# Gated linear attention and an MLP on one core: a fourth pair of units in the one-token layout, more turns by DMA, first states scaled out of PSUM, softplus for three logs, and a new order

## The chip, the core and the metric

The kernel runs on one core of a Trainium2 chip. The metric is the time of the whole program on the device in microseconds (us). Five engines work side by side, each through its own queue in order: TensorE (PE) multiplies matrices into PSUM, VectorE (DVE), ScalarE (ACT) and GpSimd (POOL) do elementwise work, and SyncE (SP) issues transfers, which 16 DMA engines carry out. ACT and DVE read PSUM; POOL and the DMA engines work on SBUF.

## The reference

A gated linear attention, whose output feeds an MLP with SiLU. There are 4 batches, 8 heads, 768 tokens and 48 columns per head; the MLP goes from 384 to 2048 and back.

```python
f = 1.0 / (1.0 + np.exp(-f_logit))
for t in range(S):
    state = f[:, :, t, :, None] * state + np.einsum('bhd,bhe->bhde', k[:, :, t], v[:, :, t])
    y[:, :, t] = np.einsum('bhd,bhde->bhe', q[:, :, t], state)
...
h = x @ w_in
g = h * (1.0 / (1.0 + np.exp(-h)))
return (g @ w_out)
```

Here x is y with the eight heads of a token side by side, 3072 rows of 384.

## The kernel before

**Units and pairs.** The 768 tokens of a batch are cut into six chunks of 128. One batch's chunk is a unit, so there are 24; they are worked in twelve pairs (`PAIRS`, line 19). In a pair of kind N the units are the same chunk of two batches, and each of the 128 partitions holds one token: a head's row in DRAM is 192 bytes. In a pair of kind T the two units are two neighbouring chunks of one batch, and a partition holds two neighbouring tokens (384 bytes); rows 0 to 63 are the first chunk's, and a step with index i takes every second token of both, so each matmul for scores, values or states comes in pieces of 64 rows. Before, pairs 0 to 3 are T (chunks 0 and 1 of the four batches) and pairs 4 to 11 are N.

**Steps of a unit.** The words are those of the plan; P is the pair and i the unit.
- f, k, q, v: loads, of a whole pair or of half of it (line 239, queue of SP).
- E, L: the log of the gate. E is exp(-f) (line 246) and L is ln(1 + E) (lines 258 and 261). Where the plan has L without E, L is one softplus(-f) (lines 249 to 255).
- cs: running sums of the logs along the tokens, by a triangular matrix on PE (lines 317 to 332). ia and a: its exp with both signs (line 334); al: the decay of a whole chunk (lines 276 and 336).
- ki, qg: k and q times these (line 339). vb: v in bf16 (line 341).
- The turned qk: eight PE transposes, tq (line 346), and a copy out of PSUM, qkc (lines 350 and 352); or one DMA transpose, qkD (line 354).
- sc: scores (lines 363 and 367). at: masked scores (line 371). y, and yi for the second unit of a T pair: the output of the unit, from the scores and from the state before it (lines 283, 379, 383). yc: y to bf16.
- d, sd, su: the change of the state (lines 295 and 400), its sum with the state before (line 404; for a first chunk a copy, line 406), and that times the decay (line 414), two instructions of 48x192. Where the plan has su without sd, su reads d in PSUM (line 411).
- The turned y: three PE transposes, yT (line 391), and a copy, xc (line 393); or one DMA transpose, yD (line 395).
- mi, si, mo, oc, so: the MLP. mi is two blocks of 128 of the hidden layer for the pair's 256 tokens (six matmuls, line 269; a third index makes it one unit's 128 tokens), si the SiLU (line 274), mo a quarter of the second product for one unit (four matmuls, line 304), oc the copy out of PSUM, so the store (lines 314 and 316).
- wi, wo: loads of the weights on POOL's queue, with a cast to bf16 (lines 216 and 219). idle: matmuls of zeros, 512 columns each (line 459).

**What sets the order.** `PLAN` (line 37) is a list written out in full, 881 words before. A word is name:engine:slots, where the engine is A (ACT), V (DVE), G (POOL), S (SP) or P (PE), and slots are the buffers taken. Instructions are emitted in this order, so each engine works through its own words in this order and waits at each for what it needs. That holds for SP too: a qkD or yD that waits keeps the loads behind it back. ACT keeps one set of tables at a time: `mode_of` (line 449) tells which of softplus, exp (with ln) and silu a step needs, and line 507 loads the set where it changes.

Of the kernel before, what the change touches and what calls it, by code (L numbers as in the profile page):

```python
# [41 lines left out]
idle.512.3::3 sc.0.0:P:3,7 al.2:A:1 ia.2.0:A:4 su.0.0:G:0 sc.0.1:P:5,1 f.4.0:S:0 at.0.0.1:V:0 E.3.0:A:0 at.0.0.0:V: tq.1.0:P:7 al.1:A:2 a.2.0:A:2
wi.1:G: v.2.0:S:2 at.0.1.0:V:1 tq.1.1:P:2 L.3.0:A:0 qkc.1.1:V:1 qkc.1.0:A: ki.2.1:G:4 idle.512.1::3 cs.3.1:P:3 at.0.1.1:V: cs.3.0:P:4 a.3.1:A:1
ki.2.0:V:0 wi.0:G: sc.1.0:P:5,2 ia.3.1:A:0 at.1.0.0:V:2 y.0:P:7,1 a.2.1:A:3 qg.2.0:G: al.3:A:3 yc.0.0:A:0 at.1.0.1:V: q.3.0:S:3 sc.1.1:P:6,3
vb.1.1:A:2 yi.0.1:P: qg.2.1:G: at.1.1.1:V:3 yT.0.0:P:5 vb.1.0:A:3 tq.2.0:P:7 yc.0.1:A:1 at.1.1.0:V: d.1:P:2,3 a.3.0:A:4 wi.2:G: yT.0.1:P:1 sd.1.0:A:1
tq.2.1:P:6 xc.0.1:V:0 ia.3.0:A:2 xc.0.0:V: su.1.0:G:0 k.3.0:S:3 y.1:P:2,1 qkc.2.0:A:0 sd.0.1:V:0 mi.0.3.0:P:4 yc.1.0:V:2 mi.0.3.1:P: wi.3:G:
qkc.2.1:V: yi.1.1:P: mi.0.2.0:P:5 yc.1.1:A:0 yT.1.0:P:0 su.0.1:G:0 mi.0.2.1:P: xc.1.0:V:1 E.4.0:A:1 yT.1.1:P:7 xc.1.1:V: sc.2.1:P:2,6 sd.1.1:V:1
sc.2.0:P:1,0 L.4.0:A:1 mi.1.2.1:P:7 at.2.1.0:V:0 mi.1.3.1:P:3 mi.1.3.0:P: at.2.0.0:V:1 k.4.0:S:4 mi.1.1.0:P:2 at.2.1.1:V: mi.1.1.1:P: mi.1.2.0:P:
at.2.0.1:V: si.0.2:A:0 mi.0.1.0:P:1 mi.0.1.1:P: si.1.1:A:1 mi.1.0.0:P:6 si.1.2:A: mi.0.0.1:P:5 vb.2.1:G:4 mi.1.0.1:P: vb.2.0:A:5 wo.0:G: mi.0.0.0:P:
# [4 lines left out]
mi.2.2:P:4 si.2.3:A:2 si.1.7:A: tq.3.1:P:7 v.4.0:S:5 si.2.0:A: mi.2.1:P:1 qkc.3.1:V:1 si.0.6:A: mo.0.1.0:P:6 si.2.1:A: vb.3.1:G:6 tq.3.0:P:3
su.2.1:G:0 si.1.6:A: mi.2.5:P:7 qkc.3.0:V: si.1.5:A: mi.2.7:P:2 vb.3.0:G:0 si.2.5:A: wo.3:G: mo.0.0.0:P:1 si.2.7:A: v.5.0:S:0 si.2.2:A: ki.4.1:G:3
d.3:P:5,0 sd.3.0:V:0 sc.3.0:P:3,7 sc.3.1:P:2,4 su.1.1:G:0 at.3.0.1:V:2 mo.0.0.1:P: at.3.1.0:V:3 E.5.0:A:0 mo.2.1.0:P:5 su.3.0:G:0 mo.1.1.0:P:7
L.5.0:A:2 f.6.0:S:2 mo.1.1.1:P: sd.3.1:V:1 at.3.1.1:V: mo.0.0.2:P: at.3.0.0:V: mo.2.1.1:P: y.3:P:2,0 mo.1.1.2:P: q.4.1:S:4 mi.2.6:P:4 mi.2.4:P:3
# [4 lines left out]
vb.5.1:A:2 mo.2.0.3:P: qkD.4.1:S:0 mi.3.1:P:7 oc.2.0:V:3 vb.4.0:V:3 mi.3.0:P:2 si.3.2:A:3 oc.2.1:V:4 si.3.3:A: qg.4.0:V: mo.1.0.2:P: si.3.5:A:
mi.3.6:P:0 q.6.0:S: ki.5.0:G:4 si.3.1:A: f.8.0:S:3 tq.4.0:P:3 si.3.0:A: so.1.1:G: mi.3.4:P:5 vb.4.1:A:4 qg.5.0:V: q.7.0:S:1 vb.6.1:A:5 qg.5.1:V:1
mo.1.0.3:P: si.3.4:A: ki.5.1:G: cs.6.1:P:1 qkc.4.0:A:1 mi.3.7:P:4 cs.6.0:P:7 si.3.7:A: d.4.0:P:2 qkD.5.0:S:2 mo.3.1.0:P:5 sd.4.0:V:0 si.3.6:A:
oc.1.0:V:5 vb.5.0:A:0 mo.3.1.1:P: sc.4.1:P:3,4 sc.4.0:P:2,0 at.4.1.0:V:0 mo.3.1.2:P: qkD.5.1:S:3 a.6.1:A:2 at.4.0.0:V:1 mo.3.0.0:P:6 E.8.0:A:0
# [475 lines left out]
```

## Time and profile before

| what | time |
| --- | --- |
| median of 3 runs | 183.14 us |
| lowest and highest run | 183.08 and 184.12 us |
| the profiled execution | 181.74 us |
| its span, first to last instruction | 179.9 us |
| mean granted TensorE clock | 0.991 of full speed |

The profile shows one execution. Its views are a page (shares of busy time, slices of the span, the chain of work that ended last, groups of like instructions) and answers about the trace: stretches of the span, the chain in order of time, waits, DMA landings. In a group's row, "x32 | 2.4, 219 | 0.0" means 32 instructions, busy 2.4 us together, 219 ns each on average, and 0.0 us during which their engine was idle just before them. "<-" after that names what ended the idle time. "pb" is any of the eight PSUM buffers. Matmuls are pipelined, so 32 of 219 ns fit into 2.4 us.

### The profile page before, as it was taken

The numbers are of one execution on the slowest core, as the hardware profiler recorded it, in microseconds if no ns is written. First come the engines' busy times: TensorE is split into PE (matmuls) and PEld (weight loads), VectorE is DVE, ScalarE is ACT, GpSimd is POOL, SyncE is SP. The second block draws the span as 40 slices with busy tenths as digits, with TensorE's granted clock in tenths as the row PEclk, the third lists the DMA queues.
The fourth block names the chain that finished last, engine by engine and source line by source line (L and its number), as shares of the span: only waits on it lengthen the run. The fifth ranks groups of instructions, "written<-read, shape, count | busy, mean of one in ns | idle before, by whom it ended". The sixth has DMA issues, their size and how long they took to land.

```text
span 179.9 us, 4982 instructions
## 1 busy us (share of the span) xinstructions
PE 170.3 (95%) x2039; PEld 130.0 (72%) x2040; DVE 83.2 (46%) x165; ACT 134.9 (75%) x252; POOL 59.9 (33%) x107
## 2 busy tenths in 40 slices
PE   6978599999999999999999999998999999999992
PEld 2355589998666787679688877787866877887782
DVE  7089977343710263793666064551058758000010
ACT  4899759999936899887997969783896971278321
POOL 6027753695200370140464500581305220003030
PEclk9999879999999999999999999999999999999999
DMA  5999999999989997999949999698985951314043
GB/s 142 315 321 309 202 242 256 230 209 193 180 176 182 203 201 134 210 204 207 158 106 221 178 202 205 125 218 170 216 156 122 213 127 26 109 26 131 0 154 112
DMA packets 109574, 31.91 MB, mean 177 GB/s; under 512 B 103536, under 2 KB 109088, under 8 KB 109552
## 3 DMA queue, kind: packets, MB, share of 16 engines
q1 hardware_dynamic: 104928, 26.19, 69.1%
q0 software_dynamic: 4624, 5.41, 16.0%
q8 instruction: 16, 0.26, 0.6%
q14 instruction: 6, 0.05, 0.1%
HBM read 25.17 MB, written 4.72 MB: 166 GB/s over the span
## 4 chain that ended last, share of the span: by engine, by line
PE 84%; ACT 6%; DVE 3%; DMA 2%; issue 2%; POOL 0%; POOLq 0%; DVEq 0%
PE pb L304 33%; PE pb L269 33%; PE pb L459 3%; DMA xT<-yb 2%; ACT x L334 2%; PE pb L346 2%; PE pb L379 2%; PE pb L383 2%; PE pb L367 2%; DVE atm L371 2%; PE pb L329 2%; DVE qk L339 1%; PE pb L391 1%; PE pb L295 1%; PE pb L363 1%
## 5 line engine op out<-in xcount | busy, mean ns | idle before, releaser
L304 PE MATMUL pb<-w_out_sb,hT 128*128 128x384 bf16 (+1 forms) x416 | 70.7, 313 | 0.1
L269 PE MATMUL pb<-xT,w_in_sb 128*128 128x256 bf16 (+1 forms) x672 | 70.1, 257 | 0.7 <-DMA xT<-yb 0.5
L274 ACT ACTIVATE hT<-pb 128x512 bf16<-128x512 f32 x96 | 51.0, 611 | 23.2 <-PE pb L269 23.1
L269 PEld LDWEIGHTS <-w_in_sb 128*128 128x128 bf16 x672 | 56.9, 98 | 8.2 <-issue 0.9
L304 PEld LDWEIGHTS <-hT 128*128 128x128 bf16 x416 | 37.9, 97 | 18.1
L414 POOL TENSOR_TENSOR st<-sd,al 48x192 bf16<-48x192 f32 x40 | 20.6, 516 | 54.7 <-PE pb L379 18.2
L371 DVE TENSOR_TENSOR atm<-pb,triu 128x512 bf16<-128x512 f32 x32 | 20.0, 682 | 15.2 <-PE pb L367 15.2
L187 DVE COPY ob<-pb 128x384 f32<-128x384 f32 (+1 forms) x16 | 8.3, 526 | 36.0 <-PE pb L304 35.9
L334 ACT ACTIVATE x<-pb 128x384 f32<-128x384 f32 x48 | 22.0, 511 | 3.3 <-PE pb L329 1.5
L507 ACT ACT_TABLE_LOAD x17 | 21.8, 1283 | 0.3
L339 POOL TENSOR_TENSOR qk<-k,x 128x384 bf16<-128x384 f32 x11 | 11.4, 1038 | 14.9 <-DVE vb L187 13.5
L339 DVE TENSOR_TENSOR qk<-k,x 128x384 bf16<-128x384 f32 x13 | 11.9, 936 | 8.3 <-DMA k<-in_k_dram 5.4
L404 DVE TENSOR_TENSOR sd<-pb,st 128x384 f32<-128x384 f32 x16 | 8.6, 550 | 12.6 <-PE pb L400 6.1
L316 POOL DMA_DIRECT2D out_dram<-ob x7 | 4.0, 569 | 29.5 <-ACT ob L185 21.1
L339 DVE TENSOR_TENSOR qk<-q,x 128x384 bf16<-128x384 f32 x17 | 11.4, 688 | 3.3 <-DMA q<-in_q_dram 1.8
L246 ACT ACTIVATE e<-f 128x768 f32<-128x768 f32 (+1 forms) x13 | 10.5, 804 | 2.0 <-DMA f<-in_f_logit_dram 2.0
L185 ACT CAST yb<-pb 128x384 bf16<-128x384 f32 x16 | 7.6, 490 | 3.6 <-PE pb L383 2.4
L371 DVE TENSOR_TENSOR atm<-pb,mask 128x512 bf16<-128x512 f32 x16 | 10.1, 680 | 0.4 <-PE pb L363 0.4
L339 POOL TENSOR_TENSOR qk<-q,x 128x384 bf16<-128x384 f32 x7 | 7.1, 1019 | 7.4 <-ACT x L334 5.8
L459 PE MATMUL pb<-zero,triu 128*128 128x512 bf16 x19 | 7.1, 525 | 1.5 <-POOL triu masks.py:66 1.4
L185 ACT COPY ob<-pb 128x384 f32<-128x384 f32 (+1 forms) x10 | 4.4, 456 | 4.6 <-PE pb L304 4.6
L346 PE MATMUL pb<-ident,qk 128*128 128x128 bf16 x80 | 6.7, 234 | 0.4 <-DVE atm L371 0.4
(72 smaller groups left out, 153.2 us busy)
## 6 DMA issues: line engine op xcount, KB each, us to landing
f<-in_f_logit_dram SPq DMA_DIRECT2D x11, 384.0 KB, 5.5
k<-in_k_dram SPq DMA_DIRECT2D x16, 192.0 KB, 3.7
v<-in_v_dram SPq DMA_DIRECT2D x16, 192.0 KB, 4.3
q<-in_q_dram SPq DMA_DIRECT2D x16, 192.0 KB, 4.2
q<-in_q_dram SPq DMA_DIRECT2D x4, 384.0 KB, 5.2
k<-in_k_dram SPq DMA_DIRECT2D x4, 384.0 KB, 4.9
v<-in_v_dram SPq DMA_DIRECT2D x4, 384.0 KB, 7.3
w_in_sb<-in_moe_w_in_dram POOLq DMA_DIRECT2D x4, 384.0 KB, 7.5
```

What stands on the lines that cost most here:

```text
L185: nc.scalar.copy(dst, src)
L246: return nc.scalar.activation(e, at("f", P)[:, j * w:(j + 1) * w], AF.Exp, scale=-1.0)
L269: nc.tensor.matmul(h[:, i, cols], w_in_sb[:, kk, n * 128:(n + 1) * 128], at("xT", P)[:, kk, cols], start=(kk == 0), stop=(kk == KT - 1))
L274: return nc.scalar.activation(at("hT", P)[:, 2 * j:2 * j + 2, :], at("h", P, j).rearrange("p (n c) -> p n c", n=2), AF.Silu)
L304: nc.tensor.matmul(at("o", P, i)[:, cols], at("hT", P)[:, n, i * C:(i + 1) * C], w_out_sb[:, n, cols], start=(n == 0), stop=(n == NT - 1))
L334: nc.scalar.activation(at(kind, P, i).rearrange("p h d -> p (h d)"), at("cs", P, i)[:, 0:HD], AF.Exp, scale=1.0 if kind == "ia" else -1.0)
L339: ENG[eng].tensor_mul(at("qk", P, i)[:, j, :, 0:D], heads("qk"[j], P, i), at("ia" if j else "a", P, i))
L346: nc.tensor.transpose(t_ps[:, j, p, :], at("qk", P, i)[:, j, 2 * p:2 * p + 2, :], ident)
L371: ENG[eng].tensor_mul(at("atm", P, i)[:, r], at(f"s{r}", P, i).rearrange("p (n c) -> p n c", c=C), mask[:, None, :].to_broadcast([C, NP, C]))
L414: ENG[eng].tensor_mul(at("st", P, i)[lo:lo + D, :, r * D:(r + 1) * D], src[lo:lo + D, :, r * D:(r + 1) * D], al_of(P, i)[lo:lo + D, :, Non ...
L459: nc.tensor.matmul(buf["pb", int(got)][:, 0:rest[0]], triu, zero[:, 0:rest[0]], start=True, stop=True, skip_group_check=True)
L507: nc.scalar.preload_act_table_set(TABLES[mode])
```

## The change

Pair 3 becomes N: the same units, (3,0) and (3,1), that is chunks 0 and 1 of batch 3, with one token per partition. Its four loads become halves, one per unit. `emit` gets a case for a load of one unit, which takes batch and chunk from the unit itself, and a case for qkD of a T pair, which the new plan doesn't use.

The plan is a new one, of 871 words. What is on PE, ACT, DVE, POOL and SP in it, by count before and after:

| steps | before | after |
| --- | --- | --- |
| tq with qkc (turn of qk on PE) | 10 | 6 (pairs 0 to 2) |
| qkD (turn of qk by DMA) | 14 | 18 |
| yT with xc (turn of y on PE) | 12 | 6 |
| yD (turn of y by DMA) | 12 | 18 |
| E on ACT | 13 | 10 (none for pairs 0 to 2) |
| L on ACT | 13 | 14 (softplus for pairs 0 to 2: four) |
| sd on ACT / DVE | 3 / 17 | 0 / 16 (none for the four first chunks) |
| su on POOL / DVE | 20 / 0 | 16 / 4 |
| ki on DVE / POOL | 13 / 11 | 18 / 6 |
| qg on DVE / POOL | 17 / 7 | 14 / 10 |
| vb on ACT / DVE / POOL | 10 / 8 / 6 | 3 / 10 / 11 |
| oc on ACT / DVE | 10 / 16 | 17 / 9 |
| so on SP / POOL | 14 / 12 | 7 / 19 |
| idle matmuls | 20 | 16 |
| table sets that ACT loads, the first included | 18 | 19 |

In the new order the pairs follow one another by number throughout, and most loads of a unit stand one pair ahead of their use. The old order loads further ahead (f.4, k.4 and v.6.1 stand before the first MLP products of pair 2, for instance), and it works pair 8 ahead of pair 7. The core of the diff, with the first lines of both plans:

```diff
-    ('T', (3, 0), (3, 1)),
+    ('N', (3, 0), (3, 1)),
...
-f.0.0:S:0 f.0.1:S: f.2.0:S:1 f.1.0:S:2 q.0.0:S:0 E.0.0:A:0 E.0.1:A: k.0.0:S:0 L.0.0:A:0 L.0.1:A: idle.512.11::0 cs.0.1:P:0 E.2.0:A:1 k.1.0:S:1
-cs.0.0:P:1 ia.0.1:A:0 v.0.0:S:0 E.1.0:A:0 ia.0.0:A:1 q.1.0:S:1 a.0.0:A:2 L.1.0:A:1 qg.0.0:G:0 L.2.0:A:2 f.3.0:S:3 idle.512.5::2 cs.1.1:P:2 ki.0.0:V:
-al.0:A:0 a.0.1:A:3 ki.0.1:V:1 cs.1.0:P:3 ia.1.1:A:4 cs.2.0:P:4 k.2.0:S:2 qg.0.1:V: ia.1.0:A:2 tq.0.0:P:5 ki.1.1:V:2 a.1.0:A:1 cs.2.1:P:6 ki.1.0:V:3
...
+f.1.0:S:0 f.0.1:S:1 f.0.0:S: q.0.0:S:0 k.0.0:S:0 L.1.0:A:0 f.2.0:S:2 L.0.1:A:1 idle.512.9::0 cs.1.1:P:0 L.0.0:A: k.1.0:S:1 cs.1.0:P:1 cs.0.0:P:2
+q.1.0:S:1 cs.0.1:P:3 ia.0.0:A:0 a.0.0:A:1 ki.0.0:V:0 v.0.0:S:0 al.1:A:0 ia.1.0:A:2 qg.0.0:V: a.0.1:A:3 ia.0.1:A:4 qg.0.1:V:1 ia.1.1:A:0 v.1.0:S:1
+idle.512.2::4 tq.0.0:P:4 ki.0.1:V: a.1.0:A:1 qkc.0.0:V:0 a.1.1:A:3 tq.0.1:P:5 ki.1.1:G:2 f.3.0:S:3 qkc.0.1:V: ki.1.0:V:3 L.2.0:A:2 q.2.0:S:2
+idle.512.3::6 sc.0.0:P:6,7 qg.1.0:V: sc.0.1:P:2,1 at.0.0.0:V:0 qg.1.1:G: cs.2.0:P:0 tq.1.0:P:4 k.2.0:S:2 at.0.1.0:V:1 cs.2.1:P:5 wi.1:G: qkc.1.0:V:1
+al.0:A:1 vb.0.1:A:0 tq.1.1:P:6 f.3.1:S: a.2.0:A:4 vb.0.0:G:1 at.0.1.1:V: qkc.1.1:A: vb.1.0:G:2 d.0:P:2,3 at.0.0.1:V: vb.1.1:G:3 v.2.0:S:2 su.0.0:V:0
+a.2.1:A:0 wi.0:G: idle.512.2::4 sc.1.1:P:4,1 ia.2.0:A:2 sc.1.0:P:7,6 at.1.1.1:V:2 E.3.0:A:0 wi.2:G: y.0:P:2,0 at.1.1.0:V: yc.0.0:A:0 yi.0.1:P: wi.3:G:
+yc.0.1:A:1 at.1.0.0:V:3 d.1:P:1,2 ia.2.1:A:1 yT.0.0:P:4 at.1.0.1:V: qg.2.1:G:4 al.2:A:2 L.3.0:A:0 yT.0.1:P:0 xc.0.0:V:0 q.3.0:S:3 cs.3.0:P:7
+su.1.0:V:0 qg.2.0:G:0 y.1:P:5,6 xc.0.1:V: yc.1.0:A:2 yi.1.1:P: sd.0.1:V:0 mi.0.3.0:P:4 al.3.0:A:3 mi.0.2.1:P:1 ki.2.1:V: yT.1.0:P:0 ki.2.0:V:
...
                 w = n * HD
+                if n == 1:
+                    b, c = us[j][0] - j, us[j][1]
...
         elif kind == "qkD":
-            nc.sync.dma_start_transpose(out=at("qkT", P, i).rearrange("p j n c -> p (j n) c"), in_=at("qk", P, i).rearrange("p j h d -> p (j h d)"))
+            if T:
+                dst = at("qkT", P).rearrange("p j n g s c -> p (j n) g s c")[:, :, :, i]
+            else:
+                dst = at("qkT", P, i).rearrange("p j n c -> p (j n) c")
+            nc.sync.dma_start_transpose(out=dst, in_=at("qk", P, i).rearrange("p j h d -> p (j h d)"))
```

A later stretch of the new plan, around the turns of pair 3: `qkD.3.0:S:0 ... v.3.0:S:3 ... v.3.1:S: ... k.3.1:S: ... vb.3.0:V:6 ... d.3.0:P:6 ... ki.3.1:V: ... qkD.3.1:S:1`, in which SP comes to v.3.0, v.3.1 and k.3.1 only behind qkD.3.0. At the end, both plans work the second product of pair 11 in halves of 192 columns, and store these.

More of the change, by code (lines that the diff above doesn't have):

```diff
@@ L42 @@
[L42 to L49, printed above, removed]
@@ L54 @@
[L54 to L57, printed above, removed]
@@ L62 @@
[L62 to L65, printed above, removed]
@@ new lines @@
+so.3.0:G: si.6.3:A: y.7.0:P:2 so.4.1:G: ki.8.0:V:2 mo.6.1.0:P:0 si.6.4:A: yc.7.0:V:0 su.6.1:G:0 mo.6.0.1:P: q.8.1:S: d.7.1:P:5 yD.7.0:S: mo.6.1.1:P:
+sd.7.1:V:0 a.8.0:A:4 mo.6.0.2:P: E.9.0:A:0 qg.8.0:V: mo.6.1.2:P: al.8.1:A:5 qkD.8.0:S:3 al.8.0:A:0 L.9.0:A:0 mo.6.1.3:P: d.7.0:P:4 qg.8.1:V:
+oc.6.1:A:1 v.8.0:S:2 cs.9.0:P:1 cs.9.1:P:2 a.9.0:A:0 mi.7.1:P:5 q.9.0:S:3 ia.9.1:A:1 ia.9.0:A:2 qkD.8.1:S:2 mi.7.0:P:3 a.9.1:A:4 al.9.1:A:4
+mo.6.0.3:P: al.9.0:A:3 sc.8.0:P:6,0 at.8.0.1:V:0 mi.7.6:P:2 k.9.0:S:3 si.7.1:A:3 at.8.0.0:V: mi.7.5:P:1 si.7.6:A: v.8.1:S: vb.8.0:V:1 mi.7.7:P:0
@@ new lines @@
+k.10.0:S: mo.8.0.3:P: L.11.0:A:2 v.10.1:S:4 d.9.1:P:4 mo.8.1.2:P: sd.9.1:V:0 so.2.0:S: qg.10.0:V:2 cs.11.1:P:7 mi.9.7:P:6 ki.10.1:V: cs.11.0:P:2
+oc.8.0:V:3 qkD.10.1:S:3 mi.9.0:P:5 a.11.0:A:1 ia.11.0:A:4 mi.9.1:P:1 a.11.1:A:2 ki.10.0:V: ia.11.1:A:0 mo.8.1.3:P: qkD.10.0:S:2 vb.10.1:V:5 mi.9.4:P:4
+mi.9.2:P:3 q.11.0:S:5 si.9.1:A:2 mi.9.6:P:2 v.10.0:S: si.9.2:A: si.9.0:A: q.11.1:S: mi.9.5:P:7 si.9.7:A: sc.10.1:P:1,3 si.9.6:A: k.11.1:S:5
+at.10.1.1:V:0 mi.9.3:P:5 oc.8.1:A:0 at.10.1.0:V: mo.9.0.0:P:6 si.9.3:A: so.8.1:G: k.11.0:S: qg.11.0:V:4 si.9.4:A: sc.10.0:P:2,3 si.9.5:A:
```

100 lines of the change are left out of this document (51 added, 49 removed).

## The prediction

> **What bounds the kernel now.** I read the page's shares of busy time first, then the slices, then three stretches of the span side by side, then the chain that ended last.
>
> ```profile
> PE 170.3 (95%) x2039; PEld 130.0 (72%) x2040; DVE 83.2 (46%) x165; ACT 134.9 (75%) x252; POOL 59.9 (33%) x107
> PE   6978599999999999999999999998999999999992
> DMA  5999999999989997999949999698985951314043
> ```
>
> TensorE (PE) is the bound by far. The row of slices says where it is not: only the first five of 40 slices (4.5 us each) hold gaps of size. The DMA engines are the second busiest thing, full until the last quarter.
>
> ```profile
> 0.00:25.17 25.17, 19.50 (x285) 12.33 (x287) 17.43 (x47) 19.55 (x41) 11.04 (x29) 0.93 1.06 259
> 25.17:176.77 151.60, 150.78 (x1760) 117.64 (x1754) 65.73 (x119) 115.09 (x212) 48.90 (x79) 1.00 0.84 166
> 176.77:179.90 3.13, 0.00 (x0) 0.00 (x0) 0.00 (x0) 0.31 (x1) 0.00 (x0) 1.00 0.26 84
> ```
>
> Columns: length, then busy us (instructions) of PE, weight loads, DVE, ACT and POOL, then granted clock, DMA share, GB/s. The kernel has three parts: a start of 25.17 us until the first MLP matmul (mi.0.3.0), a dense part in which PE is busy 150.78 of 151.60 us, and a tail of 3.13 us. So a change pays in two ways only: it takes matmuls out of the dense part, or it lets the dense part begin earlier. And it costs where it opens holes in the dense part.
>
> The chain shows what sets the start (start us, length us, what):
>
> ```profile
> 17.26 0.68 DVE atm L371
> 17.94 1.69 DVE qk L339
> 19.63 1.18 issue
> ...
> 36.88 0.17 PE pb L391 x3
> ...
> 41.19 0.45 PE pb L346 x8
> ```
>
> Up to 24.7 us it runs through ACT's exponentials and DVE's masks and products; from there it is PE alone.
>
> **The change part by part.** Counts are from the two plans.
>
> *Turns moved from PE to DMA.* tq goes from 10 to 6, yT from 12 to 6. The chain prices a tq (eight transposes in a row) at 0.45 us and a yT (three) at 0.17. In the order after the first MLP matmul the old plan has 4 tq and 10 yT, the new one 2 and 4: 2 x 0.45 + 6 x 0.17 = 1.9 us less PE. (The other two removed tq show in where the dense part begins.) As bounds, the two groups below give 2.4 / 4 = 0.60 per tq and 3.3 / 10 = 0.33 per yT, latency included: 1.9 to 3.2.
>
> ```profile
> L391 PE MATMUL pb<-ident,yb 128*128 128x128 bf16 x30 | 3.3, 219 | 0.0
> L346 PE MATMUL pb<-ident,qk 128*128 128x128 bf16 x32 | 2.4, 219 | 0.0
> ```
>
> The copies out of PSUM that go with them (four qkc, six xc), three sd and seven vb leave ACT some 8 us lighter in net; ACT is not the bound (115 of 151.6), so I count nothing. The same goes for moved oc, ki, qg and vb.
>
> *Pair 3 in the other layout.* Its score, value and state products become half as many with all rows in use; by the times in the chain these cancel within 0.2 us. I take 0.1 less, so the dense part has **2.0 us** less work in all.
>
> *The start.* Here softplus, the PSUM scaling and the new order act together, so I follow the new order along each engine.
>
> ```profile
> 4.16 0.52 ACT L246 ACTIVATE e<-f 128x384 f32<-128x384 f32 x1 [0.36 <-DMA f<-in_f_logit_dram]
> 7.12 0.49 ACT L334 ACTIVATE x<-pb 128x384 f32<-128x384 f32 x1 [0.42 <-PE pb L326]
> 9.58 1.48 DVE L339 TENSOR_TENSOR qk<-k,x 128x384 bf16<-128x384 f32 x2 [5.36 <-DMA k<-in_k_dram]
> 10.50 2.03 ACT L334 ACTIVATE x<-pb 128x384 f32<-128x384 f32 x5
> L339 DVE TENSOR_TENSOR qk<-k,x x5: 546/550/3023, 9.6 to 17.9; 128x384 bf16<-128x384 f32 x5
> L261 ACT ACTIVATE lf<-e 128x768 bf16<-128x768 f32 x8 | 6.8, 849 | 0.2
> L507 ACT ACT_TABLE_LOAD x17 | 21.8, 1283 | 0.3
> L185 ACT COPY qkTT<-pb 128x1024 bf16<-128x1024 bf16 x3 | 3.3, 1084 | 0.0
> L187 DVE COPY qkTT<-pb 128x1024 bf16<-128x1024 bf16 x5 | 3.4, 687 | 3.6 <-PE pb L346 3.6
> L185 ACT COPY sd<-pb 128x384 f32<-128x384 f32 x3 | 1.5, 512 | 2.2 <-PE pb L295 2.2
> L187 DVE COPY ob<-pb 128x192 f32<-128x192 f32 x2 | 0.7, 358 | 21.4 <-PE pb L304 21.4
> L414 POOL TENSOR_TENSOR st<-sd,al 48x192 bf16<-48x192 f32 x40 | 20.6, 516 | 54.7 <-PE pb L379 18.2 <-DVE sd L404 10.9 <-DVE qk L339 9.1
> 5.00:15.00 10.00, 8.28 (x110) 4.88 (x110) 5.01 (x10) 9.23 (x22) 1.32 (x2) 1.00 1.15 318
> ```
>
> Softplus is not in the trace. The nearest row is Ln on the same 128x768 (0.85 us); the function that it replaces needs Exp and Ln, so between 0 (free) and 1.7 (as dear as both). I take 0.85. Loads of two tokens per partition land one per 0.393 MB / 318 GB/s = 1.24 us. f.1.0, now first and whole, is as many bytes as the two first halves of before, which were in at 4.16. L.1.0 then ends at 5.0, and L.0.0 at about 6.3. A table load to exp (1.28) follows, so the first ia starts at 7.6, against 7.12. Nine operations at 2.03 / 5 = 0.41 us take ACT to 11.3. Softplus's table, L.2.0 and exp's table (3.4) take it to 14.7; al.0, vb.0.1, a.2.0 and the copy qkc.1.1 (1.08) to 16.8.
>
> DVE: k.0.0 is now the fourth such load, not the fifth, so it lands about 1.2 us earlier, near 8.3, and the first product starts there instead of at 9.58. Products at 0.55 us, held to ACT's pace, are done by 10.6; two qkc (0.69) by 12.0; ki.1.0 and qg.1.0 by 13.1, or by 14.0 if POOL's product beside them holds them up. Three at, qkc.1.0 and another at (0.68 each) end the masks of pair 0 at 16.5 to 17.4, against 17.94. Now the old order lost the most: ki.2.0 took 3.02 us, not 0.55, beside POOL's products (the maximum in the row for k above, 1.69 + 1.18 in the chain). The new order puts su.0.0 there, straight from PSUM. A DVE write of 48x192 from PSUM with two inputs isn't shown; I take 0.36 from the copy of 192 columns, bounded by 0.2 and POOL's 0.52. It replaces sd on ACT (0.5) and two su on POOL (1.0) by 0.72 on DVE. Four at (pair 1, waiting for qkc.1.1 until 17.1) end near 20.8, xc.0.0, su.1.0 and xc.0.1 near 22.2, and the first MLP matmul starts near **21.9** instead of 25.17. It isn't dense yet: tq.2.1 and tq.2.0 wait for ki.2.1 and ki.2.0 on DVE, some 1.7 us later, and yT.1.1 for a copy behind them. PE runs without a hole from 24.1 to 25.1, say 24.6, and has then done 2.1 us of the work that before lay behind 25.17. The gain is 25.17 - 24.6 + 2.1 = **2.7 us**. Bounds: 4.0 (no hole after the first MLP matmul, dense from 23.3) and 0.1 (softplus at 1.7 for three pairs, 2.55 us later).
>
> *What the turns cost.* Each qkD waits on SP's queue for ki and qg, and each yD for yc; the loads of v and k for the next units stand right behind them (qkD.3.0, then v.3.0, v.3.1, k.3.1), so a late ki delays vb and d as well.
>
> ```profile
> qkT<-qk SPq DMA_TRANSPOSE x14, 3.5
> DMA to landing us min/median/max: 2.3/2.6/5.8
> ```
> ```profile
> L185 ACT CAST yb<-pb 128x384 bf16<-128x384 f32 x16 | 7.6, 490 | 3.6 <-PE pb L383 2.4
> ```
> ```profile
> 96.81 5.89 PE pb L269 x54
> ...
> 106.97 2.60 PE pb L304 x16
> ```
> ```profile
> PE pb L269 <- DMA xT<-yb: 0.5, 1, 0.5
> ```
>
> qkD takes 3.5 us to land; the second row is yD's. I added up PE's new order between a pair's last y and its first mi, at 0.65 us per group of mi (six matmuls, 5.89 / 9) or mo (four, 2.60 / 4). What is left after a copy of 0.5 us and a landing of 2.6 us is 0.3 to 2.3 us at the boundaries of pairs 3 to 11. Nine boundaries against six, and landings that reach 5.8 us: I take **1.5 us** of new holes; from 0 to 6 (nine times 0.65).
>
> *Fewer idle matmuls, one more table load, stores from POOL, 2 or 3 halves of a load more:* nothing. ACT and POOL have the room, and the tail's last two copies and stores are as before.
>
> *Sum against the profiled execution*, 181.74 us (span 179.9, 1.84 around it): -2.0 - 2.7 + 1.5 = -3.2, so 178.5. The median of the runs, 183.14, lies 1.4 above the profiled one; from it the same sum gives **179.9 us**, rounded to 180.0.
>
> **The rivals.** *The DMA engines become the bound: slower.* Engine time per MB is share x length / bytes:
>
> ```profile
> 50.00:60.00 10.00, 10.00 (x113) 6.74 (x111) 0.96 (x2) 4.98 (x11) 0.00 (x0) 1.00 0.94 186
> 141.50:146.30 4.80, 4.80 (x45) 3.94 (x43) 2.91 (x8) 4.08 (x7) 0.00 (x0) 1.00 0.78 149
> 60.00:130.00 70.00, 69.28 (x755) 53.80 (x752) 34.22 (x64) 58.96 (x115) 26.67 (x43) 1.00 0.96 184
> ```
>
> Loads of one token per partition (50 to 60 us): 0.94 x 10 / 1.86 = 5.05 us per MB; two tokens (5 to 15 us): 1.15 x 10 / 3.18 = 3.6; turns (141.5 to 146.3): 5.2; stores (the tail's row): 3.1. A qkD of 0.262 MB is 1.4 us, a yD of 0.098 MB 0.5. The change adds 4 x 1.4 + 6 x 0.5 = 8.6 and pair 3's loads 1.57 x 1.45 = 2.3: 10.9 us of DMA time. An N pair needs 7.9 + 3.8 + 1.2 = 12.9, and PE spends 151.6 / 12 = 12.6 on a pair. Because the new order loads fewer pairs ahead, pairs 4 to 11, pair 3's turns and early stores, some 106 us, fall between about 46 and 158 us: a share of 0.95. Before, 0.96 was carried from 60 to 130 us with 0.7 us of PE gaps (69.28 busy of 70), and 1.15 was reached; so it should fit, with little over. If SP's waits let only 0.88 through, these stages take 120.5 us, 8.5 more: 183.1 - 4.7 + 8.5 = 186.9. It passes the gain where the share stays below 106 / (112 + 4.7) = 0.91.
>
> *The turns come late: no change.* Each boundary loses 0.5 us instead of 0.17, 4.5 us in all: 183.1 - 4.7 + 4.5 = 182.9. For it: a yD of before took 5.8 us to land. Against: PE waited for xT once in six pairs, 0.5 us in all. The Trainium skill speaks against this part of the change: its page "VectorE: DVE Perf Modes", section "The three transpose paths", gives a 128x128 turn as 390 ns on TensorE and 1309 ns by DMA, and says to use TensorE where PSUM is acceptable. By that rule each of ten moved turns would be a loss. The trace agrees on latency (0.45 us and a copy against 3.5) but not on cost, since PE is the bound.
>
> *The start gives nothing: no change.* If each of the three table loads ahead of qkc.1.1 also drained ACT for as long as it lasts, the chain above would be 3 x 1.28 = 3.8 us longer and all of the 2.7 gone: 183.1 - 2.0 + 1.5 + 1.1 = 183.7. In the trace 17 loads have 0.3 us of idle time before them, so I give it little. The Trainium skill, "ScalarE: Activation LUTs", section "What ACT_TABLE_LOAD costs", has this drain (1380 ns on top of 1283); the row here shows 1283 and no such idle time.
>
> **How the numbers follow.** Forecast 0.60, late turns 0.22, empty start 0.03, DMA bound 0.15. The forecast's own range is 177 to 182. With the rivals the range is 176.8 to 185.3: the lower end is 4.0 at the start, 2.0 of PE work and hardly any hole, and the upper end takes in the late turns and the beginning of the DMA rival, leaving out some 0.15. A measurement here tells 1% (1.8 us) from no change. Faster by more than that (under 181.3): 0.60. Within 1%: 0.25. Slower: 0.15.
>
> **What would show it.** The start: first MLP matmul near 22 us and PE without holes from 24 to 25; softplus near 0.85 us; su on DVE near 0.36; no DVE product of 3 us. The dense part: tq 6, yT 6, and PE's gaps there near 2 us, on xT. The DMA share near 0.95 from 46 to 158 us. Wrong if PE waits for qkT, qk or loads at several pairs, if the share saturates, or if the first MLP matmul is no earlier than 25.

## The result, and the profile after

The changed kernel takes **190.94 us** (median of 4 runs, 190.23 to 191.90) beside 183.63 us for the kernel before on the same chip (4 runs, 183.08 to 184.35): a ratio of 1.040, 95% interval 1.033 to 1.047. It is slower by 7.3 us; the prediction was 180.0 us, in a range to 185.3. The profiled execution took 191.27 us, with a span of 189.5. (Some executions of either kernel are 1 to 2% longer at random; the ratios below leave these out, so a median can lie above ratio times before.)

The page of the changed kernel, first the shares and then the slices (4.7 us each):

```profile
PE 171.8 (91%) x1944; PEld 126.9 (67%) x1944; DVE 78.9 (42%) x166; ACT 130.0 (69%) x242; POOL 60.3 (32%) x109
...
PE   7788856999999999999799999999999989997992
...
PEclk9969997999999999999999999999999999999999
DMA  6999999908989789999799999898999898837004
```

PE's row now dips where it was full: slices 6 and 7 (23.7 to 33.2 us), and in PEclk the seventh slice ran at 0.7 of the clock. (The third ran at 0.6; the kernel before has a loss of that kind in its fifth and sixth, 0.8 and 0.7.) The DMA row, which was nearly all 9 until the last quarter, has an empty slice (the ninth, 37.9 to 42.6 us).

The same three parts as in the prediction, with the dense part cut in three, for after and then for before:

```profile
0.00:21.76 21.76, 17.33 (x263) 10.40 (x264) 15.55 (x48) 16.15 (x30) 11.41 (x29) 0.92 1.01 240
21.76:45.00 23.24, 19.16 (x329) 17.03 (x327) 10.07 (x20) 13.35 (x28) 8.23 (x13) 0.93 0.90 146
45.00:165.00 120.00, 115.94 (x1160) 83.90 (x1158) 49.11 (x91) 92.09 (x170) 36.45 (x59) 1.00 0.97 187
165.00:186.13 21.13, 19.41 (x201) 15.59 (x198) 4.13 (x8) 8.09 (x17) 4.25 (x8) 1.00 0.34 99
```
```profile
25.17:45.00 19.83, 19.83 (x362) 18.41 (x357) 10.07 (x18) 18.73 (x34) 12.52 (x20) 1.00 1.23 221
45.00:155.00 110.00, 109.22 (x1207) 81.35 (x1205) 54.94 (x99) 85.95 (x157) 32.56 (x52) 1.00 0.88 173
155.00:176.77 21.77, 21.73 (x196) 17.87 (x193) 0.71 (x2) 10.40 (x22) 3.83 (x7) 1.00 0.26 80
```

The first MLP matmul does come at 21.76 us (forecast 21.9, before 25.17). But from there to the last matmul it takes 186.13 - 21.76 = 164.4 us instead of 151.6. PE stands idle for 4.08 + 4.06 + 1.72 = 9.9 us of it, as against 0.8 before. Length times GB/s gives the bytes that have moved by 45 us: before 25.17 x 259 + 19.83 x 221 = 10.9 MB, after 21.76 x 240 + 23.24 x 146 = 8.6 MB. The new order is 2.3 MB behind when its dense part has begun. Some 1.5 MB of that are missing from 31 to 45 us (14 us at 101 GB/s instead of 211), around the empty slice.

What PE waited for in the changed kernel (us in total, times, longest):

```profile
PE pb L330 <- ACT lf L262: 4.9, 3, 3.4
PE pb L347 <- DVE qk L340: 2.8, 3, 1.7
PE pb L270 <- DMA xT<-yb: 2.7, 5, 1.4
...
PE pb L372 <- DMA qkT<-qk: 1.0, 2, 0.6
```

The longest wait of the first row, 3.4 us, is cs.3.1, which waits for L.3.1 on ACT. ACT itself stood still: the last load of f ahead of it, f.3.1 (one transfer on SP's queue), is in this answer on the tile f from 14 to 32 us:

```profile
L240 SPq DMA_DIRECT2D f<-in_f_logit_dram x1: 1809/1809/1809, 15.3 to 15.3; - x1
...
  DMA f<-in_f_logit_dram: 4.9, 1
...
DMA to landing us min/median/max: 13.7/13.7/13.7
```

It went out at 15.3 us and landed 13.7 us later; the four halves of f take 4.4 us in the median, the ten whole loads, with twice the bytes, 5.2. What else was on the DMA engines then is in POOL's timeline (start, length), after and before. Lines L215 and L216 are the loads of the first weight matrix, L218 those of the second:

```profile
14.04 0.94 POOL L215 DMA_DIRECT2D w_in_sb<-in_moe_w_in_dram  x1
...
16.32 2.29 POOL L215 DMA_DIRECT2D w_in_sb<-in_moe_w_in_dram  x3
...
26.51 1.54 POOL L218 DMA_DIRECT2D w_out_sb<-in_moe_w_out_dram  x2
```
```profile
15.71 0.95 POOL L216 DMA_DIRECT2D w_in_sb<-in_moe_w_in_dram  x1
...
17.67 0.79 POOL L216 DMA_DIRECT2D w_in_sb<-in_moe_w_in_dram  x1
...
20.38 0.79 POOL L216 DMA_DIRECT2D w_in_sb<-in_moe_w_in_dram  x1
...
25.24 0.78 POOL L216 DMA_DIRECT2D w_in_sb<-in_moe_w_in_dram  x1
```

Before, the four loads of the first matrix went out over 9.5 us, with products between them that POOL had to wait for (su.1.0 ahead of the last). After, all four went out between 14.04 and 18.6 us: the new plan has three of them in a row, and su.0.0 and su.1.0, at which POOL used to wait, are on DVE. The DMA queues show the effect. From 14 to 31 us the weights' loads (POOL's queue) took 66.9% of the engines' time by their packets and moved 1.84 MB, against 55.3% and 1.53 MB before; SP's loads took 51.1% and moved 1.87 MB, against 63.6% and 2.69 MB. (Shares here can add up to more than 100%: the DMA share of this stretch is 1.19, and 1.20 before.) And the hole has a second price (two stretches of the changed kernel):

```profile
26.00:30.00 4.00, 0.70 (x13) 0.58 (x11) 0.95 (x2) 0.99 (x2) 1.99 (x3) 1.00 1.22 227
30.00:35.00 5.00, 4.89 (x70) 4.46 (x69) 1.29 (x2) 4.38 (x9) 2.72 (x5) 0.66 1.28 206
```

PE is busy for 0.70 of 4 us, with the DMA engines as full as in the fullest rows (1.22), and in the next 5 us the granted clock is 0.66.

### The profile page after: what moved, and what is told of

It reads as the page before. It is cut to its first block, busy times and chain, and to the rows that moved or that the text cites. A ratio compares the mean times of both kernels' runs of the same rounds, so it can differ in the third digit from the quotient of the medians.

```text
span 189.5 us, 4779 instructions
## 1 busy us (share of the span) xinstructions
PE 171.8 (91%) x1944; PEld 126.9 (67%) x1944; DVE 78.9 (42%) x166; ACT 130.0 (69%) x242; POOL 60.3 (32%) x109
## 3 DMA queue, kind: packets, MB, share of 16 engines
HBM read 25.17 MB, written 4.72 MB: 158 GB/s over the span
## 4 chain that ended last, share of the span: by engine, by line
PE 43%; DMA 31%; SPq 12%; issue 4%; DVE 4%; ACT 4%; POOL 1%; DVEq 0%; POOLq 0%
PE pb L270 20%; PE pb L305 16%; DMA xT<-yb 10%; SPq L240 9%; DMA f<-in_f_logit_dram 7%; DMA v<-in_v_dram 5%; DMA qkT<-qk 5%; DMA k<-in_k_dram 3%; PE pb L372 2%; SPq L359 2%; DVE qk L340 1%; PE pb L388 1%; PE pb L384 1%; SPq L400 1%; DVE sd L409 1%
## 5 line engine op out<-in xcount | busy, mean ns | idle before, releaser
L305 PE MATMUL pb<-w_out_sb,hT 128*128 128x384 bf16 (+1 forms) x416 | 69.3, 313 | 0.3 <-DVE ob L186 0.2
L376 DVE TENSOR_TENSOR atm<-pb,triu 128x512 bf16<-128x512 f32 x36 | 23.0, 683 | 21.3 <-PE pb L372 20.5
L419 POOL TENSOR_TENSOR st<-sd,al 48x192 bf16<-48x192 f32 x32 | 17.5, 548 | 31.1 <-PE pb L384 17.4
L317 POOL DMA_DIRECT2D out_dram<-ob x14 | 7.8, 559 | 32.4 <-DVE ob L186 22.6
L186 POOL CAST vb<-v 128x384 bf16<-128x384 f32 x11 | 5.4, 505 | 31.8 <-DMA v<-in_v_dram 31.8
L340 POOL TENSOR_TENSOR qk<-q,x 128x384 bf16<-128x384 f32 x10 | 10.0, 1006 | 14.2 <-DMA q<-in_q_dram 6.6
L247 ACT ACTIVATE e<-f 128x768 f32<-128x768 f32 (+1 forms) x10 | 7.8, 777 | 6.5 <-DMA f<-in_f_logit_dram 6.3
L186 DVE COPY ob<-pb 128x384 f32<-128x384 f32 (+1 forms) x9 | 4.5, 507 | 16.2 <-PE pb L305 15.8
L184 ACT COPY ob<-pb 128x384 f32<-128x384 f32 (+1 forms) x17 | 7.9, 466 | 4.2 <-PE pb L305 4.1
L340 POOL TENSOR_TENSOR qk<-k,x 128x384 bf16<-128x384 f32 x6 | 6.0, 995 | 13.5 <-DMA k<-in_k_dram 12.7
L330 PE MATMUL pb<-lf,triu 128*128 128x384 bf16 x18 | 5.5, 324 | 4.9 <-ACT lf L262 4.9
```

The source lines that it names most:

```text
L184: nc.scalar.copy(dst, src)
L186: ENG[eng].tensor_copy(dst, src)
L305: nc.tensor.matmul(at("o", P, i)[:, cols], at("hT", P)[:, n, i * C:(i + 1) * C], w_out_sb[:, n, cols], start=(n == 0), stop=(n == NT - 1))
L340: ENG[eng].tensor_mul(at("qk", P, i)[:, j, :, 0:D], heads("qk"[j], P, i), at("ia" if j else "a", P, i))
L376: ENG[eng].tensor_mul(at("atm", P, i)[:, r], at(f"s{r}", P, i).rearrange("p (n c) -> p n c", c=C), mask[:, None, :].to_broadcast([C, NP, C]))
L419: ENG[eng].tensor_mul(at("st", P, i)[lo:lo + D, :, r * D:(r + 1) * D], src[lo:lo + D, :, r * D:(r + 1) * D], al_of(P, i)[lo:lo + D, :, Non ...
```

## The experiments

Each kernel is compared with the kernel before on the same chip; a ratio below 1.040 is a gain over the changed kernel. Words are those of the plan.

**First guesses: f.3.1's place, and loads further ahead.** The first kernel moves one word (`f.3.0:S:3 f.3.1:S:` side by side), the second moves every load from v.3.0 on four turns earlier on SP, the third does both.

> The changed kernel with one load moved: f.3.1, the second half of pair 3's gate, is issued right behind f.3.0 instead of behind q.2.0 and k.2.0. Nothing else differs. Theory A (the hole at the start): PE's 3.6 us at cs.3.1 and the 2.1 us of half clock behind it come from this load, which landed 13.7 us after its issue beside the weight loads; they go, and the time falls by 4 to 5.7 us, to 185.2 to 187 us, with the holes after 60 us (about 8 us) unchanged. Rival B (DMA engines full): the time that is won at the start is lost again in later holes, and the time stays within 1.5 us of 190.9.

> The changed kernel with SP's queue in another order: each load from v.3.0 on stands four turns (qkD or yD) further ahead; bytes, slots and all other queues are as they were. Theory C (loads held back): in the changed kernel loads stand behind turns that wait for DVE or ACT, SP issues nothing from 30.7 to 42.6 us and then loads come in bursts that the next turns queue behind. With the loads ahead, d.3.0, cs.7.1 and most boundaries are on time, PE's holes after 50 us fall from about 10 us to under 4, and the time is 183 to 186 us; the hole at cs.3.1 stays. Rival B (DMA engines full): the same bytes need the same time, holes after 60 us stay over 6 us, and the time is 188 us or more.

> Both edits of order at once: f.3.1 right behind f.3.0, and each later load four turns further ahead. Theories A and C together: the two gains add, as they lie in different parts of the span: 190.9 - 5 - 6 = 180 us, between 178 and 182, below the kernel before. Rival B (DMA engines full): 186 us or more.

All three got slower: 193.39 us (ratio 1.052, 1.044 to 1.059), 197.08 (1.063, 1.052 to 1.074) and 196.12 (1.064, 1.055 to 1.073). Theories A and C fell. Rival B's times (188 us or more, 186 or more) came true in the second and third; the first lost more than its 1.5 us. What PE waited for, in the first kernel, and then in the second:

```profile
PE pb L347 <- DVE qk L340: 6.8, 2, 5.2
```
```profile
PE pb L372 <- DMA qkT<-qk: 8.0, 6, 2.8
```

With f.3.1 early the wait for it is gone and a wait of 5.2 us for the product on k of pair 2, which PE has to turn, stands in its place: k.2.0 now lands 13.9 us after its issue, at 30.3 us. With loads ahead, the turns stand behind them in SP's queue, and PE waits 8.0 us for turned qk instead of 1.0. So it isn't one word's place: what one transfer gains another loses.

**Fewer bytes in the dense part.** From pair 4 on, f brings one head of eight (the gates of seven heads are left out):

```diff
+            if kind == "f" and P > 3:
+                src = src.rearrange("s (i h) d -> s i h d", h=H)[:, :, 0]
+                dst = dst.rearrange("p (i h) d -> p i h d", h=H)[:, :, 0]
             return nc.sync.dma_start(out=dst, in_=src)
```

> The changed kernel, but the f loads of pairs 4 to 11 bring only the first head of each unit, so seven eighths of the gate's data in these pairs is left out (old data of an earlier pair is used). All queues, waits and issues are as they were; DMA work falls by 8 x 2.0 x 7/8 = 14 us. Rival B (DMA engines full): holes after 60 us fall from about 8 us to under 2, and the time to 183 to 185 us. Theory C (order on SP's queue): the holes stay over 4 us and the time is 187 us or more; only cs.7.1, which waited for f.7.0 itself, is better.

188.03 us, ratio 1.022 (1.015 to 1.028). Here is its stretch from 45 to 165 us:

```profile
45.00:165.00 120.00, 118.37 (x1205) 86.69 (x1203) 52.47 (x96) 93.69 (x173) 37.21 (x60) 1.00 0.85 166
```

PE's idle time there falls from 4.06 to 1.63 us as the DMA share falls from 0.97 to 0.85. From 45 us to the last matmul it is 3.9 us instead of 5.8, so the transfers' load costs some 2 us there, less than half of the loss. Neither theory had it whole: the holes fell as rival B has it, the time stayed above the 187 us of theory C. Part of the gain is not the cut's: from the first MLP matmul to 45 us, where no load was changed, PE idles for 2.9 us instead of 4.1. The hole is still there: f.3.1 lands after 14.0 us, and PE waits 2.9 us for the product on k instead of 3.4 at cs.3.1.

**The weights further apart.** On POOL's queue wi.2 goes behind qg.2.1, wi.3 behind su.1.1, wo.0 behind vb.2.0 and wo.2 behind vb.2.1 (POOL's words alone, without slots):

```diff
-vb.1.1 wi.0 wi.2 wi.3 qg.2.1 qg.2.0 su.1.1 wo.0 wo.2 vb.2.0 su.0.1 wo.1 vb.2.1
+vb.1.1 wi.0 qg.2.1 wi.2 qg.2.0 su.1.1 wi.3 vb.2.0 wo.0 su.0.1 wo.1 vb.2.1 wo.2
```

> The new kernel with the loads of the MLP weights further apart on POOL's queue: wi.2 behind qg.2.1, wi.3 behind su.1.1, wo.0 behind vb.2.0, wo.2 behind vb.2.1; all else as it is. Theory A2: the start hole is made by weight loads, which were issued three at a time at 16.3 to 18.6 us and two more at 26.5, and while they run SP's loads get half of the DMA engines. Then f.3.1 and k.2.0 land some 4 us earlier, the hole of 3.6 us and the half clock behind it (2.1 us) are gone, first MLP matmul stays near 21.8, time about 185.5. Rival B2: all these bytes have to come anyway by about 30 us, so the hole moves to another load or to a weight matmul and the time stays within 1.5 us of 190.9.

Ratio 1.019 (1.011 to 1.027); median 188.31, lowest 185.25. That is between the theories (185.5 would be 1.010, 190.9 is 1.040): half of the loss is gone by reordering POOL's queue alone. The landing of f.3.1 is not what theory A2 forecast: in the kernel e9_last_values below, which has these weights in the same order, it still takes 12.7 us and ends at 26.8 us, 2.2 us earlier and not 4; PE's wait for it is 1.6 us, and the clock stays at 1.00.

**Less bytes in the start, same order.** The stronger test: leave every order alone and take away bytes. wi.0, wi.2 and wi.3 bring an eighth of their columns, and the other columns are set to zero on POOL ahead of the first load (the MLP leaves out most of the hidden layer), in the changed kernel and, as a control, in the kernel before. The lines of the loads:

```diff
-nc.gpsimd.dma_start(out=w_in_sb[:, :, n * w:(n + 1) * w], in_=w_in_src[:, :, n * w:(n + 1) * w])
+u = w if n == 1 else w // 8
+nc.gpsimd.dma_start(out=w_in_sb[:, :, n * w:n * w + u], in_=w_in_src[:, :, n * w:n * w + u])
```

> The new kernel, order untouched, with three of the four loads of the first weight matrix (wi.0, wi.2, wi.3) bringing only an eighth of their columns; the rest of these columns is set to zero on POOL before the first load lands, so the MLP's result leaves most of the hidden layer out. Removed are 1.03 MB of 8.6 MB that land before 45 us. Theory W (in the start SP's loads are short of the DMA engines because the weights come beside them): k.2.0 and f.3.1 land 3 us or more earlier, the hole of 3.6 us and the half clock behind it go, ratio to the kernel before 1.00 to 1.02 instead of 1.04. Rival C (the start's chain on ACT and DVE makes these waits): ratio 1.03 or more.

> The kernel before, order untouched, with the same cut in the loads of the first weight matrix as in e13_after_small_weights (most of the hidden layer is left out). Both theories: its start has no hole that a transfer makes and its loads are 2.3 MB further at 45 us, so little changes, ratio 0.99 to 1.00. If it falls by 2% or more, the cut helps any order, and e13_after_small_weights doesn't speak for theory W.

The changed kernel falls to 182.46 us, ratio **1.000** (0.997 to 1.004); the control to 182.21, ratio 0.997 (0.993 to 1.001). So the cut is worth 7 us to the new order and nothing to the old one, whose MLP has the same zeros, so it isn't the zeros. In the new order f.3.1 now lands 8.5 us after its issue, not 13.7, and near 23 us, not 29. The stages of the new order with the cut:

```profile
20.85:45.00 24.15, 24.01 (x383) 20.73 (x381) 10.35 (x22) 17.09 (x35) 8.11 (x13) 1.00 0.93 150
45.00:155.00 110.00, 108.02 (x1095) 78.24 (x1094) 48.40 (x90) 86.74 (x159) 36.96 (x59) 1.00 0.99 191
155.00:177.07 22.07, 20.42 (x212) 16.58 (x209) 4.13 (x8) 9.26 (x19) 4.25 (x8) 1.00 0.36 101
```

The start has no hole left (24.01 of 24.15) and no loss of clock; with its chain on ACT and DVE untouched, that chain isn't what made the hole. From 45 us to the last matmul PE idles for 1.98 + 1.65 = 3.6 us instead of 4.06 + 1.72 = 5.8: the dense part gains too.

**The turns alone.** In the old order, with pair 3 as it was, units 3.0, 3.1, 4.0, 4.1, 5.1 and 6.0 get their y turned by DMA, and 4.0 and 6.0 their qk, each where its copy stood (`xc.4.1:A:1` becomes `yD.4.1:S:1`, the yT goes). Then the reverse: the changed kernel with the weights apart, and those six turns of y back on PE.

> The kernel before (order and loads as before, pair 3 still with two tokens per partition), but the six turns of y of units 3.0, 3.1, 4.0, 4.1, 5.1 and 6.0 by DMA where the copy out of PSUM was issued, and the turned qk of 4.0 and 6.0 by DMA as well: 18 turns of y and 16 of qk by DMA, as against 12 and 14. PE loses 6 x 0.17 + 2 x 0.45 = 1.9 us. Theory B: landings of 3 us and more where a copy took 0.5 open holes and the queue of SP is held back, so that the time is 185 or more. Rival P: the turns are hidden, the time is 183.7 - 1.9 = 181.8.

> The new kernel with the weights' loads further apart (as in e2_weights_apart), and with the turns of y of units 3.0, 3.1, 4.0, 4.1, 5.1 and 6.0 back on PE (three transposes, one or two PE words behind yc, and a copy on ACT), as the kernel before had them. PE work is 6 x 0.17 = 1.0 us more, the DMA engines have 6 x 0.5 = 3 us less to do and SP issues six turns of about 1.2 us less. Theory T (late turns): waits for xT at pairs 4, 5 and 6 (0.4 to 0.9 us each) go, and SP's loads behind these turns come earlier, so the time is 1 to 2.5 us below that of e2_weights_apart in ratio to the kernel before (0.985 to 1.014). Rival E (the DMA engines as a whole are the limit from 45 to 165 us): holes fall by no more than the work that is added, ratio 1.015 to 1.025.

Alone in the old order they cost 3.2% (190.90 us, ratio 1.032, 1.024 to 1.040). What PE waited for there:

```profile
PE pb L270 <- DMA xT<-yb: 7.1, 3, 4.4
```

The old order has little PE work between a pair's last y and its first mi, since a copy took 0.5 us; a landing of 3 us shows at three pairs, once with 4.4 us. In the new order it's otherwise: the six turns back on PE give 1.022 (1.013 to 1.031) beside 1.019, no gain, as rival E has it. So the turns need an order made for them, and the new one is, as far as intervals of 1% tell; theory T fell.

**Turns on another queue.** All 18 yD as `yD.3.0:A:3` and so on, issued by ACT.

> The kernel of e2_weights_apart with all 18 turns of y issued from ACT's DMA queue, at the same places of the plan, so that they neither stand behind SP's loads nor hold these back; ACT pays the issue of each turn (1.2 us on SP's queue). The DMA engines have the same work. Theory Q (SP's queue in order is the limit): landings of xT fall from 3.4 to about 2.5 us, loads of the next pair go out up to 2 us earlier, holes from 60 to 180 us fall by 3 us or more, ratio to the kernel before about 1.00. Rival E (engines' time): ratio 1.015 to 1.025. Rival A (ACT becomes the limit, 18 x 1.2 = 21.6 us more on an engine that is busy 75% of the time): ratio 1.03 or more, PE waits for ACT's copies and SiLU.

212.26 us, ratio 1.160 (1.152 to 1.169). Landings did fall as theory Q has it, to 2.6 us, but the turns' own queue (ACTq, the waits ahead of the turns: least, median and longest ns) shows the price, followed by the answer's landing line:

```profile
L400 ACTq DMA_TRANSPOSE xT<-yb x18: 1193/1196/1627, 57.4 to 192.7; - x18
L400 ACTq EVENT_SEMAPHORE  x17: 17/38/6528, 57.4 to 189.6; - x17
...
DMA to landing us min/median/max: 2.3/2.6/4.8
```

Each turn holds its queue for 1.2 us, and some wait up to 6.5 us ahead of that, with all of ACT's work behind. Rival A is right in sign. The step from 1.019 to 1.160 is some 26 us, more than all 21.6 us of issue put end to end; what ends these waits the profile doesn't name.

**The last pair's v.** v.11.0 and v.11.1 ahead of qkD.11.1, not behind both turns (the words on SP, without slots):

```diff
-qkD.11.1 qkD.11.0 v.11.0 so.8.0 v.11.1
+v.11.0 v.11.1 qkD.11.1 qkD.11.0 so.8.0
```

> The kernel of e2_weights_apart with v.11.0 and v.11.1 ahead of qkD.11.1 and qkD.11.0 on SP, not behind them. Theory: the last hole (PE waits 1.5 to 1.85 us for xT of pair 11 at about 171 us) comes from v.11.1, which goes out 4 us late behind the two turns and so makes vb, y, yc and yD late: the hole goes, ratio to the kernel before 1.5 / 184 = 0.8% lower than that of e2_weights_apart, 1.011. Rival: the turns of qk that are now behind the loads make sc.11 late by as much: ratio 1.019.

184.25 us, ratio 1.008 (1.004 to 1.012), against 1.019 with the weights apart alone: two changes of order give back 3.2 of the 4.0%. The intervals of the two kernels just touch (1.011 to 1.027 and 1.004 to 1.012), so the size of this last step is less sure than its sign. Its waits have no row for xT any more:

```profile
PE pb L347 <- DVE qk L340: 2.9, 2, 1.6
PE pb L330 <- ACT lf L262: 1.9, 2, 1.6
PE pb L372 <- DMA qkT<-qk: 1.7, 3, 0.7
```

**What is left.** Three attempts on these rows, each from that kernel: PE's words moved past ready work; q.2.0 and k.2.0 ahead of f.3.0 on SP; v.3.0, v.3.1, k.3.1 and f.4.0 ahead of qkD.3.0, which SP otherwise waits at (the empty slice).

> The kernel of e9_last_values with some words of PE moved past work that is ready: tq.2.1 and tq.2.0 behind more first MLP products of pairs 0 and 1, sc.2.1 and cs.3.1 behind mi.0.0.1 and mi.0.0.0, and mi.8.2, mi.9.3 and mi.10.5 ahead of sc.9.1, sc.10.1 and sc.11.0. For that yc.1.1 and sd.1.1 stand ahead of ki.2.1 and ki.2.0 on DVE, and xc.1.1 is on ACT. The transfers and their order are those of e9_last_values. In that kernel PE waited 1.55 us behind tq.2.1 for ki, 1.73 us ahead of cs.3.1, and 0.5, 0.8 and 0.9 us ahead of sc.9.1, sc.10.1 and sc.11.0. Theory: the loads and turns land as before and only PE stands still where it has other work, so 3 to 5 us go: ratio to the kernel before 0.98 to 0.992. Rival: the chain behind these words (the masks and SiLU of pairs 0 to 2, the turns of pair 3) is what counts, and the wait comes back at the next word: ratio 1.000 to 1.008.

> The kernel of e9_last_values with the loads q.2.0 and k.2.0 ahead of f.3.0 on SP (f.3.0 and f.3.1 follow). If the order among SP's loads is what makes tq.2.0 wait (1.55 us for ki.2.0, whose k.2.0 lands near 23 us), that wait goes and time falls by 1 us or more: ratio 1.002 or less. If bytes as a whole are short, the wait moves to cs.3.0 and cs.3.1, whose f.3.0 and f.3.1 come later: ratio 1.005 to 1.012.

> The kernel of e9_last_values with four loads (v.3.0, v.3.1, k.3.1, f.4.0: 0.98 MB) ahead of qkD.3.0 on SP, so that they go out near 30 us instead of behind a turn that SP waits for until about 42 us. By rows of the kernel before 0.98 MB is about 5 us of the DMA engines' time that then no longer has to be done in the dense part. Theory D (the dense part's holes come from that backlog: share 0.97 from 45 to 165 us): PE's waits between 45 and 165 us fall by 1.5 us or more, ratio to the kernel before 1.000 or less. Rival K (these waits come from the chain from k through the product to qkD, which is no shorter): ratio 1.004 to 1.012. Rival W (the four loads meet the weights' loads and hold up the start again): ratio above 1.012.

They gave 1.020 (1.013 to 1.026), 1.024 (1.016 to 1.032) and 1.003 (0.997 to 1.009). The first: the waits come back at the next word, as the rival has it. In the profiled executions the span less PE's busy time is the same 13.7 us (182.0 - 168.3 and 183.8 - 170.1); PE is busy 1.8 us longer, which the rival did not say and no run explains. The second: neither time was right. ACT takes its words in order, so E.3.0, waiting for f.3.0, held back the copy of y behind it, and PE waited for that at d.1 (the waits of ACT, then of PE):

```profile
ACT e L247 <- DMA f<-in_f_logit_dram: 7.2, 1, 7.2
```
```profile
PE pb L296 <- ACT yb L184: 6.8, 1, 6.8
```

The third fills the empty slice (DMA share from 31 to 45 us 1.27), but PE's idle time from 45 to 165 us is not shorter, 3.8 us against 2.2 (rows of e9_last_values, then of this one):

```profile
45.00:165.00 120.00, 117.79 (x1201) 85.36 (x1200) 52.54 (x96) 93.22 (x171) 40.28 (x66) 1.00 0.97 194
```
```profile
45.00:165.00 120.00, 116.22 (x1176) 83.60 (x1174) 51.16 (x93) 92.94 (x170) 40.01 (x66) 1.00 0.95 188
```

Theory D, a backlog of bytes as the reason of these waits, isn't borne out. The ratio can't be told from 1.008 or from 1.

**The other two parts alone**, in the old order: softplus (four E removed), and the first states from PSUM (four sd removed, su on DVE in their place).

> The kernel before with the four E of pairs 0 to 2 removed, so that their logs are softplus; order otherwise as before. Removed are four exponentials on ACT (two of 128x384 at 0.52, two of 128x768 at 0.83: 2.7 us); added are three table loads at 1.28 (3.85 us), since the logs of pairs 1 and 2 stand behind exponentials. Theory S: softplus needs the new order; alone it costs 0 to 1.5 us, time 183.5 to 185. Rival: softplus itself brings the earlier start, time below 182.5.

> The kernel before with the first states of pairs 0 to 3 scaled straight out of PSUM on DVE (sd copies gone, su on DVE in their place); order otherwise as before. ACT loses three copies of 0.5 us, DVE one, POOL four pairs of su at 1.0 us; DVE gains four pairs at 0.72. Theory: POOL's product ki.2.1 no longer stands behind su.0.0, the start is up to 1 us earlier, time 182.5 to 183.7. Rival: the start is set by DVE's products, which get longer by 0.72, time 184 or more.

Ratios 1.003 (0.997 to 1.009) and 0.996 (0.991 to 1.001): neither moves the time by itself. Softplus brought three more table loads there, as expected. No kernel of this study beats the kernel before by more than its interval.

## Why the prediction was wrong, step by step

**The step that failed** is "PE runs without a hole from 24.1 to 25.1" in *The start*: from 26 to 30 us PE was busy for 0.70 of 4 us. It failed because the sum has no term for the loads of the weights. Its line "Fewer idle matmuls, one more table load, stores from POOL, 2 or 3 halves of a load more: *nothing*" prices other moves between the queues and leaves these loads out, and *The start* gives SP's loads one rate throughout (1.24 us each). I followed the new order along ACT, DVE and PE, and did not follow POOL's queue, although the weights are on it: with su off POOL and three words in a row, four loads of weights go out within 4.6 us, just when k.2.0, f.3.1 and the next pairs' loads need the DMA engines. Shown: the cut in bytes is worth 7 us in this order (1.040 to 1.000) and nothing in the old one, and spacing the same loads is worth half of that. The Trainium skill has a statement that fits on its page "DMA: Bandwidth & Descriptors", section "Issuing engines are not separate DMA queues": transfers started by SP, ACT or POOL run on the same 16 engines and interleave. The trace agrees: half a load took 13.7 us beside the weights' loads, and 8.5 with three of these cut.

**The start's first matmul: right.** 21.76 us against 21.9. So were its terms, in these rows of the changed kernel (softplus, su, and DVE's products on k, none of which took 3 us):

```profile
L253 ACT ACTIVATE lf<-f 128x768 bf16<-128x768 f32 x2 | 1.7, 843 | 2.2 <-DMA f<-in_f_logit_dram 2.2
L419 DVE TENSOR_TENSOR st<-pb,al 48x192 bf16<-48x192 f32 x8 | 2.8, 351 | 0.3 <-PE pb L296 0.2
```
```profile
L340 DVE TENSOR_TENSOR qk<-k,x x18: 546/558/795, 8.9 to 160.8; 128x384 bf16<-128x384 f32 x18
```

0.843 us against 0.85 and 0.351 against 0.36; the longest product on k took 0.795. Some of the fit is luck: the first ia started at 8.07 us, not 7.6, and the first product on k at 8.91, not 8.3, and the chain caught up. But an early first matmul is no gain when the next ones wait.

**"The turns cost 1.5 us of new holes": too low, and not the largest part.** Waits for xT and qkT are 2.7 + 1.0 us, against 0.5: 3.2 more. The longest, 1.4 us, is yD.11.1's, late because v.11.1 stood behind two turns (with v.11 ahead of them the wait is gone): I named that order for pair 3, and didn't price it for the last pair, where little covers it.

**"2.0 us less PE work": less than half came.** At full clock (e9_last_values) PE's whole busy time without the idle matmuls is 168.3 - 5.9 = 162.4 us; before, it was 170.3 - 7.1 = 163.2: 0.8 us less. The turns did go (by the groups, 6.7 to 3.9 and 4.3 to 1.8 us). By the rows, "these cancel within 0.2 us" for pair 3 does not hold for the scores (before, then after):

```profile
L367 PE MATMUL pb<-qkT 48*128 48x128 bf16 x128 | 5.0, 217 | 0.0
```
```profile
L372 PE MATMUL pb<-qkT 48*128 48x128 bf16 x144 | 7.1, 218 | 1.0 <-DMA qkT<-qk 1.0
```

An eighth more matmuls take 2.1 us more; pair 3's T scores saved 0.5 to 0.8. But a group's busy time also shifts with what runs beside it: the second product of the MLP, 416 matmuls in both kernels, has 70.7 us before and 69.3 after. So where the missing 1.2 us of the gain went stays open; that the new order puts the two units' scores apart is one guess, and no run tests it.

**The rivals.** "The DMA engines become the bound" had the sign and the engines, but not the place: the share from 45 to 165 us did reach 0.97 (needed 0.95), and that stretch lost 3.3 us (4.06 us idle against 0.78 from 45 to 155 before); a little more was lost between the first MLP matmul and 45 us (4.08 us idle against none), with the clock's loss on top, where I had let the engines be free. "The turns come late" is real in the old order (3.2%) and small in the new one. "The start gives nothing" came true, not by table loads (18 of them with 0.3 us of idle time).

**What stays open:** why e9_last_values, with an earlier start, is still 0.8% over. PE idles for 2.9 us by 45 us and 2.2 until 165. Its waits there are for products on k (2.9 us) and their turns (1.7), and for logs of the gate (1.9), and moving words or loads around these gave nothing. Nor did a run try pair 3's layout alone: what its halved loads add to the crowding in the start isn't separated from the rest.

## What to carry to other kernels

When a change makes one engine's queue shorter, ask what stands at its end and starts earlier for it: here the weights' loads, which nobody waits for yet, took the DMA engines from loads that PE did wait for. An early first matmul says little; add up the bytes that must have landed for the next twenty matmuls, from all queues together. And to tell a shortage of bytes from a chain, cut bytes in both kernels without touching an order: one run and one control settled what four reorderings could not.
